# Stage 1 of a two-weight spectral filter in four row tiles, with x loaded in quarters of the partitions from two queues

## The chip, the cores and the metric

The kernel runs on one core of a Trainium2 chip. A core has a matrix engine (PE, with its weight loads shown separately as PEld), a vector engine (DVE), a scalar engine (ACT), a general engine (POOL) and a queue engine (SP), each with its own instruction stream, and sixteen DMA engines that they share. On-chip memory is SBUF (128 partitions); PE writes to PSUM, which has eight banks of 512 float32 values per partition. The metric is device time of one execution in microseconds (us). Of three timed runs of the kernel before, the median is 121.32 us (121.32 to 121.65).

## The reference

One input x of 2048 rows by 1024 columns, two complex weight arrays of 2048 by 513, one gate vector of 1024. All are bf16; the transforms are computed in float32.

```python
def f(x, w_r, w_i):
    X = rfft2(x.astype(float32))
    X = X * (w_r + 1j * w_i)
    return irfft2(X, s=(2048, 1024)).astype(bfloat16)

x = A_x
g = sigmoid((x * gate_w).sum(-1, keepdims=True))
out = g * f(x, A_w_r, A_w_i) + (1 - g) * f(x, B_w_r, B_w_i)
```

Both filters are applied to the same x, so the forward transform is made once.

## The kernel before, in words

The two transforms are split into stages that are matrix products with constant matrices. The 2048 rows of x are taken as 32 times 64: a row's number is 64 n1 + 16 b + r, with n1 from 0 to 31, b from 0 to 3 and r from 0 to 15. Stage 1 is the transform over n1. Stage 2 is the transform along the columns, stage 4 the one over the 64 values of (b, r). Products with the weights follow on DVE (L504), stage 5 (L600) begins the way back, and stages 6 and 7 make the output rows.

x is loaded as 128 partitions of 16 consecutive rows: partition p = 4 n1 + b holds rows 16 p to 16 p + 15, one after the other. The loads go in four chunks c of four values of r, each in the parts that XPARTS (L293) lists, all on SP's queue. A constant M of 128 by 2048 (L46) holds, for each r, a 128 by 128 matrix that applies the transform over n1 to all four b at once: in the row of a partition with one b, the columns of the other three b are zero. M comes in three loads (`mload`, L299), the first on ACT's queue. After x and M, SP issues F2, the gate row, CK, SM and then the 44 loads of the weights (`wload`, L319), in the order in which they are used.

Before stage 1, each part of x is folded on DVE (`fold`, L333): sums (h = 0) and differences (h = 1) of columns d and 1023 - d, 256 columns at a time (s = 0, 1), into XF, which holds two chunks. `negate` (L354) makes the negated M: chunks 0 and 1 on ACT, 2 and 3 on DVE.

`stage1(c)` (L364) makes for each (h, j) of a chunk a unit of two PSUM banks. For each of its four r, two matmuls (s = 0, 1) accumulate 256 columns, M and its negative side by side; the stationary operand is 128 columns of the folded x. When a unit is complete, ACT copies it as bf16 into FT (L391), 1024 elements per partition; two of the sixteen units are copied by DVE (L389), and the very last is copied in two pieces, the first 32 of its 128 columns alone. The tag "F1a" lets the first work of stage 2 (`fold3`, L432, on DVE, and `stage2`, L442) start when that first piece is copied.

The program keeps for every engine the order in which instructions are written, and waits by semaphores for what each instruction reads or overwrites. So a matmul that waits for folded x holds back every later matmul, and an eviction that waits holds back every later ACT instruction. Steps 0 to 15 then follow (`step`, L643): stage 4 of one piece, an exchange of real and imaginary halves by DMA (`swap`, L487, on POOL's queue, for the later pieces on SP's, behind the weight loads), stage 2 of the next piece but one, and products. A stage-4 result goes into one of seven buffers, which come free when the products that read them are done.

Of the kernel before, what the change touches and what calls it, by code (L numbers as in the profile page):

```python
# [6 lines left out]
ALU = mybir.AluOpType  # L7
# [17 lines left out]
def make_consts():  # L25
# [20 lines left out]
    C["M"] = M.reshape(128, 2048)  # L46
# [186 lines left out]
def bass_gated_mix__spectral_gfnet__spectral_gfnet__prompt_kernel(nc, A_x, A_w_r, A_w_i, B_x, B_w_r, B_w_i, gate_w, out):  # L233
# [46 lines left out]
    xv = x2.rearrange("(p r) d -> p (r d)", r=16)  # L280
# [12 lines left out]
    XPARTS = {0: ((0, 1), (1, 1), (2, 2)), 1: ((0, 2), (2, 2)), 2: ((0, 2), (2, 2)), 3: ((0, 2), (2, 2))}  # L293
# [5 lines left out]
    def mload(eng, c0, n):  # L299
        load(f"M{c0}", MM, c0 * 512, n * 512, cst["M"].ap()[:, c0 * 512:(c0 + n) * 512], eng=eng, w=[("M", c) for c in range(c0, c0 + n)])  # L300

    mload("act", 0, 1)
    for c in range(4):
        t, o = xloc(c)
        for q0, n in XPARTS[c]:
            dma("sp", f"x{c}{q0}", sl(t, o + q0 * 1024, [(1, n * 1024)]), xv[:, (4 * c + q0) * 1024:(4 * c + q0 + n) * 1024], w=[("x", c, q0)])
        if c < 2:
            mload("sp", 1 + c, 1 + c)
# [3 lines left out]
    P.add("act", lambda e: e.activation(sl(DUM, 1, [(1, 1)]), sl(DUM, 0, [(1, 1)]), ACT.Sigmoid), r=["DUM"], w=["DUM2"])  # L312
# [41 lines left out]
    def negate(c, n=1, eng="act"):  # L354
        dst, src = sl(MM, 2048 + c * 512, [(1, n * 512)]), sl(MM, c * 512, [(1, n * 512)])
        kw = dict(r=[("M", k) for k in range(c, c + n)], w=[("NM", k) for k in range(c, c + n)])
        if eng == "dve":
            P.add("dve", lambda e: e.tensor_scalar(out=dst, in0=src, scalar1=-1.0, scalar2=None, op0=ALU.mult), **kw)
        else:
            P.add("act", lambda e: e.activation(dst, src, ACT.Copy, scale=-1.0), **kw)  # L360

    cnt = 0

    def stage1(c):  # L364
        nonlocal cnt
        us = [(cnt + k) % 4 for k in range(4)]
        cnt += 4
        parts = XPARTS[c] if c == 0 else ((0, 4),)
        for q0, n in parts:
            for h in range(2):  # L370
                for j in range(2):
                    u = us[2 * h + j]
                    for q in range(q0, q0 + n):
                        r = 4 * c + q
                        base = (c % 2) * 4096 + q * 1024 + h * 512
                        o = ps(u * 1024 + q * 256, [(1, 256)])
                        for s in range(2):
                            lh = sl(XF, base + 256 * s + 128 * j, [(1, 128)])
                            rh = sl(MM, r * 128, [(2048 * s, 2), (1, 128)])
                            P.add("pe", lambda e, o=o, lh=lh, rh=rh, s=s: e.matmul(o, lh, rh, start=(s == 0), stop=(s == 1)),  # L380
                                  r=[("xf", c % 2, q, h, s ^ j), ("M", c), ("NM", c)], w=[bank(2 * u + q // 2)])
                    if q0 + n < 4:
                        continue
                    for m0, mn in ((0, 32), (32, 96)) if (c, h, j) == (3, 1, 1) else ((0, 128),):
                        src = ps(u * 1024 + m0, [(128, 2), (1, mn), (256, 4)])
                        dst = sl(FT, h * 8192 + j * 2048 + 16 * m0 + 4 * c, [(4096, 2), (16, mn), (1, 4)])
                        kw = dict(r=[bank(2 * u), bank(2 * u + 1)], a=[("F1", h, j)] + [("F1a", h, j)] * (m0 == 0))
                        if (c, h, j) in ((2, 1, 1), (3, 0, 1)):
# [5 lines left out]
    negate(1)  # L394
    folds(0)
    folds(1)
    negate(2, 2, "dve")
    stage1(0)
    stage1(1)
    fold(2, 0, 2, 0)  # L400
# [520 lines left out]
```

## Time and profile before

| what | us |
|---|---|
| median of three runs | 121.32 |
| the profiled execution, its own time | 121.57 |
| span of its trace | 119.4 |
| stage 1, first fold to last eviction | 4.71 to 22.07 |
| PE busy | 110.0 |
| DVE busy | 97.4 |
| ACT busy | 98.8 |

The trace is of one execution, so sums made from its rows are compared with 121.57 us. PE's ends are modelled, because matmuls overlap in the array: a row's duration is from the start of an instruction to its result, and the spacing of starts tells the rate. The waits name what an engine waited for last. "SPq" and "ACTq" are the time in which an engine's queue issued a DMA; the transfer itself is told apart from it.

### The profile page before, as it was taken

Reading aid. Unit: us, or ns where it says so; the run is one execution under the profiler, and the core shown is the slowest. Engines: PE = TensorE matmul, PEld = TensorE weight load, DVE = VectorE, ACT = ScalarE, POOL = GpSimd, SP = SyncE. Lnnn points to the kernel's source line nnn. Section 1 sums busy time; section 2 is a strip of 40 time slices with the busy share of each in tenths; the row PEclk is TensorE's granted clock in tenths of the full one; section 3 lists DMA queues with packets and bytes.
Section 4 is the critical chain, followed back from the end, with each engine's and each line's share of the span. In section 5 each row is a group of like instructions: output and inputs, shape, how many; then the busy total and the mean of one; then the engine's idle time right before and its main releaser. Section 6 shows DMA issues by size and latency. Waiting matters only on the chain.

```text
span 119.4 us, 4238 instructions
## 1 busy us (share of the span) xinstructions
PE 110.0 (92%) x1812; PEld 88.2 (74%) x1812; DVE 97.4 (82%) x202; ACT 98.8 (83%) x119; POOL 33.9 (28%) x43
## 2 busy tenths in 40 slices
PE   6789999999999999889999999999889899999950
PEld 4566889887665766378999999999877667877420
DVE  0478998985999999999999997994537868999980
ACT  4239998999799999849999999996878968889720
POOL 1000030026664600000000000000006979789940
PEclk9999999999999999999999999999999999999999
DMA  2999999999999999844599800000000242442546
GB/s 89 314 347 412 422 379 354 350 348 349 366 362 371 361 364 363 315 150 144 128 328 401 294 4 5 0 0 5 0 5 0 96 181 88 181 176 93 206 173 236
DMA packets 17683, 26.14 MB, mean 219 GB/s; under 512 B 2113, under 2 KB 11073, under 8 KB 17665
## 3 DMA queue, kind: packets, MB, share of 16 engines
q1 hardware_dynamic: 16368, 23.00, 55.3%
q0 software_dynamic: 864, 2.36, 5.4%
q10 hardware_dynamic: 432, 0.52, 1.3%
q8 instruction: 14, 0.23, 0.8%
q14 instruction: 5, 0.03, 0.1%
HBM read 17.48 MB, written 4.19 MB: 182 GB/s over the span
## 4 chain that ended last, share of the span: by engine, by line
PE 30%; SPq 28%; POOL 12%; DMA 8%; DVE 8%; issue 6%; ACT 3%; POOLq 1%; DVEq 0%; ACTq 0%
SPq L284 28%; PE PS L600 25%; POOL MM L829 9%; DMA W<-in_B_w_i_dram 5%; DMA W<-in_A_x_dram 3%; POOL XF L829 3%; DVE W L504 3%; DVE FT L824 2%; PE PS L380 2%; DVE MM L788 2%; POOLq L860 1%; PE PS L748 1%; PE PS L777 1%; PE PS L477 1%; ACT XF L485 1%
## 5 line engine op out<-in xcount | busy, mean ns | idle before, releaser
L600 PE MATMUL PS<-CL,W 128*128 128x128 bf16 x512 | 32.4, 225 | 0.3 <-DVE W L504 0.2
L600 PEld LDWEIGHTS PS<-CL,W 128*128 128x128 bf16 x512 | 31.7, 145 | 1.3 <-DVE W L504 0.9
L829 POOL TENSOR_TENSOR MM<-FT 128x512 bf16<-128x512 f32 x14 | 17.5, 1277 | 50.9 <-DVE FT L824 50.9
L611 ACT ACTIVATE W<-PS 128x1024 bf16<-128x1024 f32 (+1 forms) x30 | 28.5, 1036 | 1.2 <-PE PS L600 1.1
L504 DVE TENSOR_TENSOR W<-XF,W 128x1024 bf16<-128x1024 bf16 (+2 forms) x36 | 22.1, 631 | 1.3 <-ACT XF L485 1.1
L504 DVE TENSOR_TENSOR W<-MM,W 128x1024 bf16<-128x1024 bf16 (+2 forms) x36 | 22.0, 636 | 0.4 <-DMA MM<-XF 0.2
L777 PE MATMUL PS<-FT,W 128*128 128x256 bf16 (+1 forms) x132 | 20.0, 302 | 0.9 <-DVE MM L788 0.4
L761 ACT ACTIVATE W<-PS 128x1024 bf16<-128x1024 f32 (+1 forms) x16 | 15.8, 994 | 3.5 <-PE PS L748 3.3
L477 PE MATMUL PS<-XF,CK 128*128 128x512 bf16 (+1 forms) x72 | 17.5, 357 | 0.8 <-ACT XF L485 0.8
L485 ACT ACTIVATE XF<-PS 128x1024 bf16<-128x1024 f32 x15 | 16.2, 1078 | 2.5 <-DVE W L504 2.1
L466 ACT ACTIVATE XF<-PS 128x1024 bf16<-128x1024 f32 x16 | 17.1, 1076 | 0.6 <-PE PS L460 0.5
L777 PEld LDWEIGHTS PS<-FT,W 128*128 128x128 bf16 x132 | 12.1, 98 | 6.7 <-DVE MM L788 0.7
L341 DVE TENSOR_TENSOR XF<-W 128x512 bf16<-128x512 bf16 (+2 forms) x34 | 11.4, 403 | 6.2 <-DMA W<-in_A_x_dram 5.9
L380 PE MATMUL PS<-MM,XF 128*128 128x256 bf16 x128 | 14.9, 273 | 1.5 <-DVE XF L341 1.4
L380 PEld LDWEIGHTS PS<-MM,XF 128*128 128x128 bf16 x128 | 12.2, 98 | 4.2 <-DVE XF L341 2.7
L391 ACT ACTIVATE FT<-PS 128x1024 bf16<-128x1024 f32 (+2 forms) x15 | 13.1, 1012 | 0.9 <-PE PS L380 0.9
L284 POOL DMA_DIRECT2D MM<-XF x18 | 9.9, 551 | 13.7 <-PE PS L477 8.1
L824 DVE TENSOR_TENSOR FT<-PS,XF 128x512 f32<-128x512 f32 x18 | 11.5, 683 | 2.3 <-ACT XF L784 2.1
L451 PEld LDWEIGHTS PS<-F,FT 128*128 128x128 bf16 x128 | 8.4, 98 | 3.1 <-ACT FT L391 0.2
L784 ACT ACTIVATE XF<-PS 128x512 f32<-128x512 f32 (+1 forms) x16 | 8.8, 547 | 1.9 <-PE PS L777 1.9
L451 PE MATMUL PS<-F,FT 128*128 128x128 bf16 x128 | 10.2, 219 | 0.0
L477 PEld LDWEIGHTS PS<-XF,CK 128*128 128x128 bf16 x72 | 4.8, 97 | 6.5 <-ACT XF L485 5.4
(63 smaller groups left out, 100.4 us busy)
## 6 DMA issues: line engine op xcount, KB each, us to landing
W<-in_A_x_dram SPq DMA_DIRECT2D x7, 512.0 KB, 7.6
out_dram<-MM SPq DMA_DIRECT2D x10, 256.0 KB, 2.7
MM<-XF POOLq DMA_DIRECT2D x18, 128.0 KB, 5.3
FT<-c_U SPq DMA_DIRECT2D x1, 2048.0 KB, 9.5
MM<-XF SPq DMA_DIRECT2D x14, 128.0 KB, 2.5
W<-in_A_w_r_dram SPq DMA_DIRECT2D x4, 256.5 KB, 6.1
W<-in_A_w_i_dram SPq DMA_DIRECT2D x4, 256.5 KB, 6.6
W<-in_B_w_r_dram SPq DMA_DIRECT2D x4, 256.5 KB, 7.0
```

Source lines behind the costliest of these rows:

```text
L284: return P.add(eng, lambda e: e.dma_start(dst, src), dma=name, **kw)
L380: P.add("pe", lambda e, o=o, lh=lh, rh=rh, s=s: e.matmul(o, lh, rh, start=(s == 0), stop=(s == 1)), r=[("xf", c % 2, q, h, s ^ j), ("M", c ...
L451: P.add("pe", lambda e, o=o, cs=cs, j=j, t=t, rh=rh: e.matmul(o, fblock(1 + cs, j, t), rh, start=(j == 0), stop=(j == 1)), r=[("F1a" if p ...
L466: P.add("act", lambda e: e.activation(dst, src, ACT.Copy), **kw)
L477: P.add("pe", lambda e, o=o, kind=kind, pm=pm, m=m, rh=rh: e.matmul(o, sl(CK, fbo(kind, pm, m), [(1, 128)]), rh, start=(m == 0), stop=(m = ...
L485: P.add("act", lambda e: e.activation(dst, src, ACT.Copy), **kw)
L504: P.add("dve", lambda e: e.tensor_tensor(out=rows((1 - h) * 64 * RP + sw * HW), in0=sl(xt, xo + 128 * h + 64 * h0, [(0, 2), (256, 4 * ni), ...
L600: P.add("pe", lambda e, o=o, l0=l0, ab=ab: e.matmul(o, sl(W, HW * ab + l0, [(RP, 128)]), sl(CL, KIo[ab], [(1, 128)]), start=(ab == 0), sto ...
L611: P.add("act", lambda e: e.activation(dst, src, ACT.Copy), r=b, a=keys)
L761: P.add("act", lambda e, s=src, d=dst: e.activation(d, s, ACT.Copy), **kw)
L777: P.add("pe", lambda e: e.matmul(ps(col, [(1, n * 256)]), lh, rh, start=(k == 0), stop=(k == last)), r=[("Y", r), "DI"] + ["DJ"] * (full o ...
L829: P.add("pool", lambda e, s=s, op=op: e.tensor_tensor(out=ods(s, 0, 2), in0=pv[:, :, 0, :], in1=pv[:, :, 1, :], op=op), r=[("PQ", pk, 0), ...
```

## The change

x is loaded in another layout: partition 32 b + n1 holds rows 64 n1 + 16 b to 64 n1 + 16 b + 15, so each b has 32 partitions of its own. A part of a chunk is now four transfers of 32 partitions, one for each b (g in the code); those of b = 2 and 3 are issued by ACT for chunks 0 to 2, and all four by SP for chunk 3. Chunk 2 is one part of four rows instead of two parts of two. M keeps only the columns of its partition's own b, so it is 128 by 512 instead of 128 by 2048, comes in one load on ACT's queue, and is negated once, on DVE, ahead of the first fold. The activation that brings the table for Sigmoid moves behind ACT's loads of chunk 1.

Stage 1 takes 32 partitions at a time: 512 matmuls with 32 rows and 64 columns instead of 128 with 128 rows and 256 columns, consecutive ones on different quarters of the rows. A call has four banks, one for each b, and two calls alternate. There are eight calls: two rows r with both h in chunk 0, and four rows with one h in the other chunks. After each call come two evictions of two banks, 1024 elements each, fifteen on ACT and one on DVE (chunk 3, h = 0). The tag "F1a" and the copy in two pieces are gone.

```diff
-    C["M"] = M.reshape(128, 2048)
+    C["M"] = M.sum(-1).swapaxes(0, 1).reshape(128, 512)
...
-    xv = x2.rearrange("(p r) d -> p (r d)", r=16)
+    xsrc = lambda r, n, g: AP(x2.tensor, x2.offset + (16 * g + r) * D, [[64 * D, 32], [1, n * D]])
...
-    XPARTS = {0: ((0, 1), (1, 1), (2, 2)), 1: ((0, 2), (2, 2)), 2: ((0, 2), (2, 2)), 3: ((0, 2), (2, 2))}
+    XPARTS = {0: ((0, 1), (1, 1), (2, 2)), 1: ((0, 2), (2, 2)), 2: ((0, 4),), 3: ((0, 2), (2, 2))}
...
-    def mload(eng, c0, n):
-        load(f"M{c0}", MM, c0 * 512, n * 512, cst["M"].ap()[:, c0 * 512:(c0 + n) * 512], eng=eng, w=[("M", c) for c in range(c0, c0 + n)])
-
-    mload("act", 0, 1)
+    load("M", MM, 0, 512, cst["M"].ap(), eng="act", w=["M"])
     for c in range(4):
         t, o = xloc(c)
         for q0, n in XPARTS[c]:
-            dma("sp", f"x{c}{q0}", sl(t, o + q0 * 1024, [(1, n * 1024)]), xv[:, (4 * c + q0) * 1024:(4 * c + q0 + n) * 1024], w=[("x", c, q0)])
-        if c < 2:
-            mload("sp", 1 + c, 1 + c)
+            for g in (0, 2, 1, 3):
+                dma("act" if g > 1 and c < 3 else "sp", f"x{c}{q0}", sl(t, o + q0 * 1024, [(1, n * 1024)], p0=32 * g, np_=32), xsrc(4 * c + q0, n, g),
+                    **({"a": [("x", c, q0)]} if g else {"w": [("x", c, q0)]}))
+        if c == 1:
+            P.add("act", lambda e: e.activation(sl(DUM, 1, [(1, 1)]), sl(DUM, 0, [(1, 1)]), ACT.Sigmoid), r=["DUM"], w=["DUM2"])
...
-    def negate(c, n=1, eng="act"):
...
+    P.add("dve", lambda e: e.tensor_scalar(out=sl(MM, 512, [(1, 512)]), in0=sl(MM, 0, [(1, 512)]), scalar1=-1.0, scalar2=None, op0=ALU.mult), r=["M"], w=["NM"])
     cnt = 0
 
-    def stage1(c):
+    def stage1(c, q0, nq, hs, engs):
+
         nonlocal cnt
...
+        s0 = 4 * (cnt % 2)
+        cnt += 1
+        w = 128 * len(hs)
+        for q in range(q0, q0 + nq):
+            for h in hs:
                 for j in range(2):
...
+                    for s in range(2):
+                        for g in range(4):
+                            lh = sl(XF, (c % 2) * 4096 + q * 1024 + h * 512 + 256 * s + 128 * j, [(1, 128)], p0=32 * g, np_=32)
+                            rh = sl(MM, (4 * c + q) * 32, [(512 * s, 2), (1, 32)], p0=32 * g, np_=32)
+                            o = ps((s0 + g) * 512 + (q - q0) * w + (h - hs[0]) * 128 + j * 32, [(64, 2), (1, 32)])
                             P.add("pe", lambda e, o=o, lh=lh, rh=rh, s=s: e.matmul(o, lh, rh, start=(s == 0), stop=(s == 1)),
...
+        for g, eng in zip((0, 2), engs):
+            src = ps((s0 + g) * 512, [(512, 2), (1, w), (w, nq)])
+            dst = sl(FT, hs[0] * 8192 + 16 * g + 4 * c + q0, [(16, 2), (64, w), (1, nq)])
...
-    negate(0)
-    negate(1)
     folds(0)
     folds(1)
-    negate(2, 2, "dve")
-    stage1(0)
-    stage1(1)
-    fold(2, 0, 2, 0)
-    fold(2, 2, 2, 0)
-    fold(2, 0, 4, 1)
+    for q0 in (0, 2):
+        stage1(0, q0, 2, (0, 1), ("act", "act"))
+    for hh in range(2):
+        stage1(1, 0, 4, (hh,), ("act", "act"))
+    folds(2)
     folds(3)
-    stage1(2)
-    stage1(3)
+    for hh in range(2):
+        stage1(2, 0, 4, (hh,), ("act", "act"))
+    for hh in range(2):
+        stage1(3, 0, 4, (hh,), ("act", ("dve", "act")[hh]))
```

More of the change, by code (lines that the diff above doesn't have):

```diff
@@ L311, in bass_gated_mix__spectral_gfnet__spectral_gfnet__prompt_kernel @@
     load("CK", CK, 0, 1056, cst["CK"].ap(), w=["CK", "GW2"])
-    P.add("act", lambda e: e.activation(sl(DUM, 1, [(1, 1)]), sl(DUM, 0, [(1, 1)]), ACT.Sigmoid), r=["DUM"], w=["DUM2"])
     dma("sp", "SM", SM[:], cst_sm.ap(), w=["SM"])
@@ L352, in folds @@
             fold(c, q0, n, h)
-    def negate(c, n=1, eng="act"):
[L355 to L360, printed above, removed]
+    P.add("dve", lambda e: e.tensor_scalar(out=sl(MM, 512, [(1, 512)]), in0=sl(MM, 0, [(1, 512)]), scalar1=-1.0, scalar2=None, op0=ALU.mult), r=["M"], w=["NM"])
@@ L362, in bass_gated_mix__spectral_gfnet__spectral_gfnet__prompt_kernel @@
     cnt = 0
-    def stage1(c):
+    def stage1(c, q0, nq, hs, engs):
         nonlocal cnt
[L366 to L370, printed above, removed]
-                for j in range(2):
[L372 to L388, printed above, removed]
-                            P.add("dve", lambda e, s=src, d=dst: e.tensor_copy(d, s), **kw)
-                        else:
-                            P.add("act", lambda e, s=src, d=dst: e.activation(d, s, ACT.Copy), **kw)
@@ L393, in bass_gated_mix__spectral_gfnet__spectral_gfnet__prompt_kernel @@
-    negate(0)
-    negate(1)
+        s0 = 4 * (cnt % 2)
[3 more added lines that the diff above has]
+            for h in hs:
+                for j in range(2):
+                    for s in range(2):
[3 more added lines that the diff above has]
+                            o = ps((s0 + g) * 512 + (q - q0) * w + (h - hs[0]) * 128 + j * 32, [(64, 2), (1, 32)])
+                            P.add("pe", lambda e, o=o, lh=lh, rh=rh, s=s: e.matmul(o, lh, rh, start=(s == 0), stop=(s == 1)),
+                                  r=[("xf", c % 2, q, h, s ^ j), "M", "NM"], w=[bank(s0 + g)])
@@ new lines, in stage1 @@
+        for g, eng in zip((0, 2), engs):
+            src = ps((s0 + g) * 512, [(512, 2), (1, w), (w, nq)])
+            dst = sl(FT, hs[0] * 8192 + 16 * g + 4 * c + q0, [(16, 2), (64, w), (1, nq)])
+            kw = dict(r=[bank(s0 + g), bank(s0 + g + 1)], a=[("F1", h, j) for h in hs for j in range(2)])
+            if eng == "dve":
+                P.add("dve", lambda e, s=src, d=dst: e.tensor_copy(d, s), **kw)
+            else:
+                P.add("act", lambda e, s=src, d=dst: e.activation(d, s, ACT.Copy), **kw)
@@ L438, in fold3 @@
             P.add("dve", lambda e, dst=dst, src=src, op=op: e.tensor_tensor(out=dst, in0=src[0], in1=src[1], op=op),
-                  r=[("F1a" if i < 2 else "F1", cs, j) for cs in css for j in range(2)] + [("FR", i, j) for j in range(2)],
+                  r=[("F1", cs, j) for cs in css for j in range(2)] + [("FR", i, j) for j in range(2)],
                   w=[("E", i, cs, s) for cs in css] + [("FR", i - 2, s)] * (i > 1))
@@ L451, in stage2 @@
                         P.add("pe", lambda e, o=o, cs=cs, j=j, t=t, rh=rh: e.matmul(o, fblock(1 + cs, j, t), rh, start=(j == 0), stop=(j == 1)),
-                              r=[("F1a" if p < 2 else "F1", cs, j), "F2"], w=[bank(b0 + t % 2)])
+                              r=[("F1", cs, j), "F2"], w=[bank(b0 + t % 2)])
         if 1 in ab:
```

## The prediction

> **What bounds the kernel now.** I read the page's busy shares first: PE 92%, ACT 83%, DVE 82%, an average over stages, so it names no bound. The slices of DMA traffic come next; the first and third lines below show stages 1 to 4 with the sixteen DMA engines full. The windows answer gives the rate: 363 GB/s while x and the constants load (2 to 15 us), 359 GB/s while the weights load (18 to 48 us).
>
> ```profile
> DMA  2999999999999999844599800000000242442546
> GB/s 89 314 347 412 422 379 354 350 348 349 366 362 371 361 364 363 315 150 144 128 328 401 294 4 5 0 0 5 0 5 0 96 181 88 181 176 93 206 173 236
> ...
> 2.00:15.00 13.00, 11.52 (x91) 8.82 (x90) 8.80 (x27) 8.38 (x12) 0.00 (x0) 1.00 0.99 363
> 18.00:48.00 30.00, 29.96 (x461) 21.48 (x459) 27.48 (x56) 28.50 (x33) 9.88 (x18) 1.00 1.08 359
> ```
>
> Then the chain of work that ended last. From 7 to 43 us it is SP issuing loads; the last weight load lands at 48.88 us and a product on DVE starts 0.05 us later; then DVE, ACT and from 54.55 us PE, without a hole to 85.7 us.
>
> ```profile
> 43.06 5.78 DMA W<-in_B_w_i_dram
> 48.88 0.04 issue
> 48.93 0.78 DVE W L504 x2
> 49.73 0.45 DVE W L504
> 50.20 2.13 DVE W L504 x6
> 52.38 0.05 issue
> 52.43 1.03 ACT XF L485
> 53.46 0.05 issue
> 53.51 1.04 PE PS L477 x4
> 54.55 10.79 PE PS L600 x176
> ```
>
> The DVE timeline shows what that chain hides: DVE runs products back to back from 31.18 us, and the one starting at 48.93 waited about 0.2 us where its neighbours start 0.1 us late anyway. So two chains arrive together at 49 us: the loads, and the compute chain that began with stage 1. The loads are later by about 0.1 us. A change to stage 1 shifts the end by the later of the two.
>
> What sets stage 1 itself is read from the ACT timeline: evictions one after the other.
>
> ```profile
> 7.48 0.63 ACT L360 ACTIVATE MM<-MM 128x512 bf16<-128x512 bf16 x1 [2.32 <-DMA MM<-c_M]
> 8.49 11.11 ACT L391 ACTIVATE FT<-PS 128x1024 bf16<-128x1024 f32 x12 [0.38 <-PE PS L380]
> 20.07 2.00 ACT L391 ACTIVATE FT<-PS 128x1024 bf16<-128x1024 f32 x3 [0.47 <-PE PS L380]
> 21.94 0.20 ACT L514 ACTIVATE CK<-PS 128x8 bf16<-128x8 f32 x1
> ```
>
> Twelve in 11.11 us with a last one of 1.06 us is a step of 0.914 us. PE is nearly as full there: eight matmuls an eviction at 256 columns, 92 of them in 10.45 us, 0.91 us per eviction. It is a tie, so a faster PE alone gives stage 1 little.
>
> **Bytes.** x is 4.194 MB and M was 0.524 MB; M becomes 0.131 MB. Before 2 us 0.03 MB had moved (windows of 1 us). Before: 4.69 MB in 12.9 us at 363 GB/s. After: 4.29 MB. At the same 363 it would take 11.8 us, 1.1 less. But each x transfer now covers 32 partitions, from two queues, and the trace has no such transfer of any size. Bounds: as fast as now (-1.1 us), or, if a quarter of the partitions reaches only half of what the engines can write, 182 GB/s: 23.6 us (+10.7). The nearest row is the weight loads: 64 partitions, 128 to 256 KB each, rows of a strided source, 359 GB/s; the x pieces are 64 to 256 KB. I take 350 for the smaller pieces: 12.3 us, 0.6 less. Everything behind x on the queues (F2, the gate row, CK, SM, 44 weight loads) moves with it, since the DMA engines never run dry: SP issues 20 x pieces where it issued seven loads of x and two of M in some 5.8 us. At 0.43 us each (median of its x issues) they take 8.6 us, so the first weight load is issued at about 11.1 us instead of 8.41. By then some 3.2 of 5.0 MB are moved, 5 us of work is queued, and this lateness costs nothing; if transfers were to drain faster than they are issued it would cost up to 2.7 us. The gate row's copy on POOL (16.84 us, 1.15 long) follows its load; PE's first instruction after stage 1 needs it at 20.6, so 2.6 us of lateness would show nowhere.
>
> [...]
>
> **ACT.** Removed: two negations of 0.63 us, both ahead of the first eviction and in waiting time, so nothing. Added ahead of the evictions: twelve x issues. M is issued by 1.10 us (0.35 us row); ten issues at 0.40 (between that row and SP's 0.43) to 5.1; the table load of 1.28 and the activation of 0.20, now behind them, to 6.6; two more issues, 7.4 if they wait for the table load, 6.6 if not. The first call (x rows 0 and 1) could be evicted when its last piece is in: issued at 2.3 us, landing after between 1.8 us (the XST row) and 4.0 us (the two 256 KB loads), 4.1 to 6.3, I take 5.5; four folds at 0.21 (eight took 1.70) 6.4; matmuls 0.6: 7.0. So the evictions begin at 7.2 us (6.6 to 8.5) instead of 8.49. ACT does 15 whole evictions where it did the work of 14: one goes from DVE to ACT. Same 1024 elements, so the same 0.914 and 1.06: 7.2 + 14 x 0.914 + 1.06 = 21.06 us. Behind the issues nothing but evictions waits on ACT; PE waits for those through the banks.
>
> **The tail.** Before, the first quarter of the last eviction alone let the second half's folds for stage 2 start: eight took 1.77 us from 20.52, a step of 0.21, the fifth at 21.37 us. Now both evictions of the last call must end: 21.06 + 0.05. That is 0.3 us earlier.
>
> **PE.** 128 matmuls of 256 columns become 512 of 64 columns on 32 rows. Nearest row: stage 6, 64 matmuls of 64 rows by 64 columns start 1.04 us apart as a block.
>
> ```profile
> 88.66 1.11 PE L748 MATMUL PS<-FT,W 64*128 64x64 bf16 x64
> 89.70 2.35 PE L777 MATMUL PS<-FT,W 128*128 128x256 bf16 x16
> ```
>
> 16.2 ns each with two row tiles; L460's full rows at 64 columns take 32.5 (eight in 0.26). Four tiles: 8.1 if they scale, 32.5 if not; I take at most 16.2, or 1.04 us a call against 1.83 us of evictions. PE is then idle half of stage 1, which is worth nothing while ACT sets the pace. At 32.5 it is 2.08 a call: PE is the bound.
>
> **DVE.** One negation of 512 instead of 1024 (0.42 us, at most) now comes before the first fold and waits for M, which is first on its queue (landing 4.5 us before): hidden by the wait for x, at worst 0.4 us into ACT's slack. One eviction less, 1.22 us; the other is done before ACT's. Folds are the same elements; those of chunk 3 need x complete by about 16 us (ACT reaches it at 18.2), at 350 GB/s it is in by 14.3. The clock was granted at 1.0 in every window.
>
> **Sum.** Compute chain -0.3; with the loads 0.6 earlier the 0.1 us on DVE goes too: -0.4 us. Against the profiled execution, 121.57 us (span 119.4, 2.2 outside): 121.2. The median of the runs is 121.32: 120.9 us. About 0.3% (0.36 us) is what a measurement can tell from no change, so this is only just outside.
>
> **Rivals.**
> x loads slower than now. The end follows the loads, us for us: they decide from 4.29 MB in 13.3 us, 323 GB/s, and below this it is slower. For it: smaller pieces, each in a quarter of the partitions, and the last 1 MB from SP alone. Against: the weight loads on half the partitions hold 359. At 290: 14.8 us, +1.9, 123.2 us. [...]
> ACT held by its issues. If an issue takes 0.6 us (the weight loads on SP do), ten take 6 instead of 4 and the last two 1.2: evictions from 9.8, +2.2 us, 123.5. It is slower once the first eviction starts after 7.96 us. Against: simple issues cost 0.35 to 0.45.
> Row tiles that do not run side by side: seven calls of 2.08 from 8.0 us to 22.6, two evictions 1.97: 24.5 against 21.37, 124.4 us. Against: the stage 6 row.
> Nothing measurable: first eviction between 7.3 and 7.96 us; the gain is the tie of PE and ACT in stage 1, 121.2.
>
> **How the numbers follow.** Forecast 0.43. Nothing measurable 0.14. x loads at 250 to 323 GB/s 0.20, half rate 0.10, ACT late 0.08, row tiles one by one 0.05. So faster 0.43, same 0.14, slower 0.43. The lower end: evictions from 6.6 us, -1.0, 120.3, and a little, 120.2. The upper end 125.0 takes in row tiles one by one and loads down to 259 GB/s; left out are half rate (0.10) and some 0.08 at both ends. The likeliest case's own range is 120.2 to 121.0.
>
> **What the profile after would show.** Loads right: 345 GB/s or more from 2 to 14 us and the last weight landing before 48.5; wrong: slices under 320 there and DVE waiting for weights at 44 to 52 us. ACT right: first eviction at 7.2, steps of 0.91, no idle time until 21. PE right: matmul blocks of under 1.05 us with idle time behind each. Slower evictions, or a granted clock below 1.0 now that PE is half idle, would be causes that I leave out of the sum.

## The result

The kernel after takes 132.57 us (median of four runs, 131.89 to 134.21), the one before on the same chip 121.41 us. The ratio is 1.090 (95% interval 1.083 to 1.097), without the slowest of the four runs of after, which was in a slower state: 9% slower, far outside the range of 120.2 to 125.0. The profiled execution of after took 132.03 us with a span of 129.8, against 121.57 and 119.4: 10.4 us to explain.

### The profile page after: what moved, and what is told of

The parts are those of the page before. It is cut to its first block, busy times and chain, and to the rows that moved or that the text cites. A ratio compares the mean times of both kernels' runs of the same rounds, so it can differ in the third digit from the quotient of the medians.

```text
span 129.8 us, 5020 instructions
## 1 busy us (share of the span) xinstructions
PE 109.3 (84%) x2196; PEld 86.8 (67%) x2196; DVE 96.2 (74%) x199; ACT 99.1 (76%) x117; POOL 34.0 (26%) x43
## 4 chain that ended last, share of the span: by engine, by line
PE 53%; DVE 20%; issue 8%; ACT 7%; DMA 6%; ACTq 3%; DVEq 0%
PE PS L586 23%; DVE W L490 14%; PE PS L763 12%; DMA W<-in_A_x_dram 6%; PE PS L734 5%; PE PS L463 4%; ACT FT L378 4%; PE PS L369 4%; ACTq L284 3%; PE PS L437 2%; DVE MM L774 2%; PE PS L446 1%; DVE XF L469 1%; DVE XF L339 1%; PE PS L504 1%
## 5 line engine op out<-in xcount | busy, mean ns | idle before, releaser
L369 PE MATMUL PS<-MM,XF 32*128 32x64 bf16 x512 | 11.8, 227 | 12.1 <-issue 6.0
L378 ACT ACTIVATE FT<-PS 128x1024 bf16<-128x1024 f32 x15 | 14.4, 1029 | 9.1 <-PE PS L369 9.1
L369 PEld LDWEIGHTS PS<-MM,XF 32*128 32x128 bf16 x512 | 8.8, 114 | 15.4 <-issue 7.0
L463 PE MATMUL PS<-XF,CK 128*128 128x512 bf16 (+1 forms) x72 | 18.3, 372 | 0.8 <-ACT XF L471 0.8
L471 ACT ACTIVATE XF<-PS 128x1024 bf16<-128x1024 f32 x15 | 16.2, 1078 | 3.1 <-DVE W L490 1.6
L437 PE MATMUL PS<-F,FT 128*128 128x128 bf16 x128 | 11.4, 236 | 1.2 <-ACT FT L378 1.2
L437 PEld LDWEIGHTS PS<-F,FT 128*128 128x128 bf16 x128 | 9.3, 106 | 4.4 <-ACT FT L378 1.4
```

The costliest lines, as they stand in the source:

```text
L378: P.add("act", lambda e, s=src, d=dst: e.activation(d, s, ACT.Copy), **kw)
L437: P.add("pe", lambda e, o=o, cs=cs, j=j, t=t, rh=rh: e.matmul(o, fblock(1 + cs, j, t), rh, start=(j == 0), stop=(j == 1)), r=[("F1", cs, j ...
L463: P.add("pe", lambda e, o=o, kind=kind, pm=pm, m=m, rh=rh: e.matmul(o, sl(CK, fbo(kind, pm, m), [(1, 128)]), rh, start=(m == 0), stop=(m = ...
L471: P.add("act", lambda e: e.activation(dst, src, ACT.Copy), **kw)
```

## The profile after

Three lines of the slices of after (40 slices of 3.25 us; PEclk is the granted clock of the matrix engine in tenths, 9 is 90% or more):

```profile
PEclk9985555555599999999999999999999999999997
DMA  3899999999999999443226992000000025443447
GB/s 114 279 313 294 283 286 347 353 347 322 336 349 322 340 293 364 162 151 134 86 83 175 402 393 90 0 5 0 5 0 5 0 88 209 173 146 129 167 158 246
```

Two things are new. From the fourth to the eleventh slice, 10 to 36 us, the matrix engine has half its clock. And the second to sixth slices move 279 to 313 GB/s where the kernel before reached 314 to 422, though the DMA engines are as full. The windows give both as means (columns: stretch, length, busy time of PE, PEld, DVE, ACT and POOL with counts, then clock, DMA share and GB/s):

```profile
2.00:15.00 13.00, 8.47 (x219) 5.24 (x217) 6.34 (x21) 5.77 (x7) 0.00 (x0) 0.76 0.96 289
18.00:48.00 30.00, 22.81 (x513) 17.64 (x510) 18.47 (x45) 22.35 (x25) 7.86 (x13) 0.70 1.05 337
```

289 GB/s instead of 363 while x loads, at a share of 0.96 instead of 0.99: the engines are as busy and move a fifth fewer bytes.

The evictions of stage 1 in the timeline of ACT (start, length, what, count, and in brackets the idle time before with its releaser):

```profile
7.84 1.98 ACT L378 ACTIVATE FT<-PS 128x1024 bf16<-128x1024 f32 x2 [0.43 <-PE PS L369]
11.38 1.97 ACT L378 ACTIVATE FT<-PS 128x1024 bf16<-128x1024 f32 x2 [1.57 <-PE PS L369]
14.66 1.94 ACT L378 ACTIVATE FT<-PS 128x1024 bf16<-128x1024 f32 x2 [1.31 <-PE PS L369]
18.50 3.77 ACT L378 ACTIVATE FT<-PS 128x1024 bf16<-128x1024 f32 x4 [1.90 <-PE PS L369]
24.30 2.86 ACT L378 ACTIVATE FT<-PS 128x1024 bf16<-128x1024 f32 x3 [2.03 <-PE PS L369]
29.02 1.94 ACT L378 ACTIVATE FT<-PS 128x1024 bf16<-128x1024 f32 x2 [1.86 <-PE PS L369]
```

The first starts at 7.84 us, 0.65 earlier than before, and each still takes its 0.9 to 1.0 us. But where the kernel before had twelve in a row without a gap, ACT now stands idle ahead of every group, 9.1 us in all, always for PE. The last one ends at 30.96 us instead of 22.07. So 8.9 of the 10.4 us are lost inside stage 1, and the engine that sets it is no longer ACT. The other 1.5 us come behind stage 1; the section on the experiments returns to them with the half clock.

What PE waited for is in its own timeline:

```profile
13.21 1.30 PE L369 MATMUL PS<-MM,XF 32*128 32x64 bf16 x44 [1.44 <-DVE XF L339]
16.56 2.66 PE L369 MATMUL PS<-MM,XF 32*128 32x64 bf16 x116 [2.05 <-issue]
19.67 0.23 PE L369 MATMUL PS<-MM,XF 32*128 32x64 bf16 x2 [0.45 <-ACT FT L378]
20.49 0.34 PE L369 MATMUL PS<-MM,XF 32*128 32x64 bf16 x9 [0.59 <-ACT FT L378]
23.35 1.77 PE L369 MATMUL PS<-MM,XF 32*128 32x64 bf16 x117 [2.52 <-issue]
25.47 0.23 PE L369 MATMUL PS<-MM,XF 32*128 32x64 bf16 x2 [0.34 <-ACT FT L378]
26.30 0.29 PE L369 MATMUL PS<-MM,XF 32*128 32x64 bf16 x8 [0.59 <-ACT FT L378]
28.06 0.92 PE L369 MATMUL PS<-MM,XF 32*128 32x64 bf16 x54 [1.47 <-issue]
```

Until 15 us PE waits for folded x. Then come three waits put down to "issue": no semaphore that the profile knows was missing. Two of them fall inside a call, after nine matmuls and after eight, so they are no waits for data. Count the matmuls from one to the next: 116 + 2 + 9 = 127, and 117 + 2 + 8 = 127. The first comes after 64 + 64 + 32 + 44 = 204 matmuls of stage 1. A hole at the same count, whatever place of the work it falls on, suggests that the engine ran out of instructions; the experiments test it. 127 matmuls with their weight loads are 254 instructions. The chain that ended last shows the same three holes, and then the old work, shifted (start, length, what):

```profile
14.51 2.05 issue
...
20.83 2.52 issue
...
26.59 1.47 issue
...
65.38 10.81 PE PS L586 x176
```

That last row stood at 54.55 us before: +10.8. The weights no longer matter; in their place this chain runs through DVE's products without a transfer in it.

The page counts the transfers that bring instructions as a queue of their own. Of the kernel before (packets, MB, share):

```profile
q8 instruction: 14, 0.23, 0.8%
```

and of after:

```profile
q8 instruction: 17, 0.28, 0.9%
```

A packet is 0.28 MB / 17, about 16.5 KB. Stage 1 went from 128 to 512 matmuls, which with their weight loads is 768 more instructions; three more packets of 256 are 768. So a packet holds 256 instructions by estimate, and the 254 from one hole to the next are nearly one packet. Up to the first hole PE ran the 18 matmuls at the program's start (L297) and 204 of stage 1, 444 instructions with their loads; why the first hole comes there is not shown.

## The experiments

Theory I: PE consumes its 512 small matmuls faster than the instruction queue delivers them while the DMA engines are full; the half clock follows from the holes (the second half of this did not hold, see below). Theory L: the slower loads of quarters set stage 1. The table gives the outcome; every ratio is to the kernel before in the same job.

| kernel | median us | ratio (95%) | x, 2 to 15 us, GB/s | PE waits put to issue in stage 1, us |
|---|---|---|---|---|
| after | 132.57 | 1.090 (1.083 to 1.097) | 289 | 6.0 |
| after_whole_loads | 130.19 | 1.067 (1.060 to 1.074) | 361 | 6.0 |
| before_quarter_loads | 126.55 | 1.040 (1.036 to 1.045) | 275 | 0 |
| after_two_tiles | 126.55 | 1.041 (1.035 to 1.048) | 287 | 0 |
| before_split_columns | 128.48 | 1.056 (1.050 to 1.063) | 375 | 3.9 |
| two_tiles_contiguous_loads | 122.10 | 1.002 (0.998 to 1.005) | 394 | 0 |

**One cause at a time.** after_whole_loads is the kernel after with x loaded as before, so that rows stand in other partitions than the row tiles assume; the instructions from stage 1 on are those of after:

```diff
-            for g in (0, 2, 1, 3):
-                dma("act" if g > 1 and c < 3 else "sp", f"x{c}{q0}", sl(t, o + q0 * 1024, [(1, n * 1024)], p0=32 * g, np_=32), xsrc(4 * c + q0, n, g),
-                    **({"a": [("x", c, q0)]} if g else {"w": [("x", c, q0)]}))
+            dma("sp", f"x{c}{q0}", sl(t, o + q0 * 1024, [(1, n * 1024)]), xv[:, (4 * c + q0) * 1024:(4 * c + q0 + n) * 1024], w=[("x", c, q0)])
```

> The changed kernel with x loaded as before: transfers of 128 partitions from SP alone, no x transfer from ACT. The rows then stand in other partitions than the four row tiles assume, so the output is not the reference's; all instructions of stage 1 and after are those of the changed kernel. Theory I (PE runs out of instructions: with the DMA engines full, a block of some 256 PE instructions takes 5 to 7 us to arrive, and 512 matmuls with their 512 weight loads use one up in 2 us; the idle PE then drops to the half clock): loads are back at about 363 GB/s, but the holes of 1.5 to 2.5 us that PE spends on 'issue' in stage 1 stay, the clock falls to 0.5 all the same, and the time is 127 to 131 us. Theory L (the slower quarter loads, 290 GB/s from 2 to 17 us, set the length of stage 1): 121 to 123 us, no holes.

x came at 361 GB/s again, the three holes stayed after the same counts (116, 2 + 9, 117, 2 + 8), and so did the half clock (0.50 in the mean of 17 to 30 us). Loads alone are not the cause.

before_quarter_loads is the reverse: the kernel before, with x in quarters from two queues. As in the change, the activation for Sigmoid moves behind ACT's loads of chunk 1; those lines are not printed here.

```diff
-            dma("sp", f"x{c}{q0}", sl(t, o + q0 * 1024, [(1, n * 1024)]), xv[:, (4 * c + q0) * 1024:(4 * c + q0 + n) * 1024], w=[("x", c, q0)])
+            for g in (0, 2, 1, 3):
+                dma("act" if g > 1 and c < 3 else "sp", f"x{c}{q0}", sl(t, o + q0 * 1024, [(1, n * 1024)], p0=32 * g, np_=32), xsrc(4 * c + q0, n, g),
+                    **({"a": [("x", c, q0)]} if g else {"w": [("x", c, q0)]}))
```

> The kernel before with x alone loaded as in the change: four transfers of 32 partitions for each part, those of the upper two quarters from ACT for chunks 0 to 2. M with its zeros and the 128 matmuls of 256 columns stay; the rows stand in other partitions than M assumes, so the output is not the reference's. Theory I: 4.69 MB at 290 GB/s take 16.2 us instead of 12.9, so the weights land 3.3 us later: 123 to 126 us, no hole on 'issue' in PE's stage 1, clock 1.0. Theory L: 130 to 133 us.

Its first window and its evictions:

```profile
2.00:15.00 13.00, 9.23 (x56) 6.52 (x55) 6.42 (x21) 4.81 (x7) 0.00 (x0) 0.87 0.98 275
```

```profile
12.93 11.11 ACT L394 ACTIVATE FT<-PS 128x1024 bf16<-128x1024 f32 x12 [3.12 <-PE PS L383]
24.34 2.00 ACT L394 ACTIVATE FT<-PS 128x1024 bf16<-128x1024 f32 x3 [0.30 <-PE PS L383]
```

The evictions run without a hole again and are 4.3 us later; the last weight landed at 53.47 instead of 48.88, the span grew by 4.7. So quarters cost 4% by themselves, and the span grew by about as much as the last weight came later.

after_two_tiles keeps the quarters and halves the number of matmuls: two row tiles of 64 partitions, two b in each, 256 matmuls of 128 columns. M is then 128 by 1024, half of it zeros.

```diff
-                        for g in range(4):
+                        for g in range(2):
...
-                            rh = sl(MM, (4 * c + q) * 32, [(512 * s, 2), (1, 32)], p0=32 * g, np_=32)
+                            rh = sl(MM, (4 * c + q) * 64, [(1024 * s, 2), (1, 64)], p0=64 * g, np_=64)
```

> The changed kernel with two row tiles of 64 rows instead of four of 32: 256 matmuls of 128 columns, M with half zeros (128 x 1024); x loads as in the change; everything is computed. Theory I: half the PE instructions, 512 in stage 1, so the holes are fewer and shorter: 123 to 128 us. Theory L: M is 0.13 MB longer and the loads are the same, so 132 to 133 us.

No wait on PE is put down to issue and the granted clock is 1.0 in every window to 20 us. The queue of instructions has 15 packets, one more than before, for 256 instructions more. Stage 1 ends at 26.31, and the whole kernel costs what the quarters alone cost.

**Is it the number of instructions, or the row tiles?** before_split_columns has neither row tiles nor new loads, only each matmul cut in four by columns:

```diff
-                        for s in range(2):
+                        for k in range(4):
+                            for s in range(2):
+                                o = ps(u * 1024 + q * 256 + 64 * k, [(1, 64)])
...
+                                rh = sl(MM, r * 128 + 2048 * s * (k // 2) + 64 * (k % 2), [(1, 64)])
```

> The kernel before with each of the 128 matmuls of stage 1 cut in four of 64 columns (512 matmuls on all 128 rows; same loads, same constants, same evictions): the number of instructions of the kernel after without its row tiles and without its loads. By theory I the number of instructions alone brings the waits for instructions: PE shows waits put down to issue inside stage 1, about 127 matmuls apart, of 1.5 to 2.5 us each, and the time is 124 to 129 us. Rival, the row tiles themselves bring them: no such waits, and matmuls at 32.5 ns each (512 take 16.6 us where 128 took 13.9 with 11.7 us of busy time) make PE the bound of stage 1 by about 2.7 us: 124.0 us, with PE back to back and the clock at 1.0.

PE's timeline:

```profile
5.34 7.01 PE L381 MATMUL PS<-MM,XF 128*128 128x64 bf16 x204 [0.66 <-DVE XF L341]
13.79 3.88 PE L381 MATMUL PS<-MM,XF 128*128 128x64 bf16 x127 [1.43 <-issue]
19.99 5.42 PE L381 MATMUL PS<-MM,XF 128*128 128x64 bf16 x127 [2.33 <-issue]
25.57 1.75 PE L381 MATMUL PS<-MM,XF 128*128 128x64 bf16 x54 [0.16 <-issue]
```

204, 127, 127, 54: the same counts as in the kernel after, without row tiles and with whole loads. So the holes go with the number of matmuls, as theory I has it. The arrival of an instruction is in no row of the traces; what follows reads the holes by that theory. Blocks arrive 6.2 and 5.6 us apart here, 6.8 and 4.7 in the kernel after. By that reading a block of 127 matmuls must last that long or PE waits. In before it lasts 127 x 0.114 = 14.5 us (eight matmuls in 0.91); with two tiles, 32 matmuls in ACT's 1.83, it lasts 7.3 us, just enough; with four, 64 in 1.83, it is 3.6 us.

**What makes a block slow?** after_weights_held makes the weights' loads wait until the last matmul of stage 1.

```diff
-                    dma("sp", f"w{key}", d, s, a=[("W", key)])
+                    dma("sp", f"w{key}", d, s, a=[("W", key)], after=[P.ops["pe"][-1]])
```

> The changed kernel with the 44 weight loads held until the last matmul of stage 1 is done, so that the DMA engines have nothing but x, F2, the gate row, CK and SM until then. The whole is longer, since the weights come later; only stage 1 is looked at. Theory I: once x has landed the blocks of instructions arrive quickly: the holes on 'issue' after 18 us (2.5 and 1.5 us) shrink below 0.7 us each and the last eviction of stage 1 ends 2 to 4 us earlier than 30.96 us. Theory L, or a limit of PE's own issue: the holes stay and stage 1 ends at 30 to 31 us.

A single execution took 137.71 us, since the weights come late. PE's timeline at the first two blocks:

```profile
17.55 2.66 PE L369 MATMUL PS<-MM,XF 32*128 32x64 bf16 x116 [2.63 <-issue]
...
22.70 1.77 PE L369 MATMUL PS<-MM,XF 32*128 32x64 bf16 x117 [0.88 <-issue]
```

The first hole, with x still loading, is no shorter (2.63 us, 2.05 in the kernel after); the second shrank from 2.52 to 0.88, the third went. PE's own pace between the first hole and the second was the same (4.3 us for these 127 matmuls in both kernels). From 17 to 30 us the DMA engines moved 83 GB/s at a share of 0.31 here, and 344 GB/s at 1.09 from 18 to 30 us in the kernel after. So, by this one execution, the other transfers lengthen the arrival of a block. It is still 5.2 us here, part of it beside x; the time of a block with nothing beside it is not shown.

**How much is the half clock?** after_fillers puts four long matmuls ahead of each call from the second on, to keep PE busy:

```diff
+        for _ in range(4 if cnt > 1 else 0):
+            P.add("pe", lambda e: e.matmul(ps(s0 * 512, [(1, 512)]), sl(MM, 0, [(1, 128)]), sl(MM, 0, [(1, 512)]), start=True, stop=True),
+                  r=["M"], w=[bank(s0)])
```

> The kernel after with four matmuls of 128 rows by 512 columns of M, whose results are overwritten, ahead of each of the calls of stage 1 from the second on (28 more matmuls, nothing else). What it tells apart: how much of the 10.6 us that the change costs is PE's halved clock, and how much the waits for instructions. Theory I with the clock as a side effect: the fillers keep PE busy ahead of the calls, the granted clock rises from 0.50 to near 1.0 in stage 1, the three waits for instructions stay (about as long, 1.5 to 2.5 us each), and the time falls by 1 to 3 us, to 129.5 to 131.5. Rival, the clock is the cause of most of the loss: with the clock near 1.0 the last eviction of stage 1 ends by 25 us instead of 30.96, and the time is 126 us or less. If the clock stays at 0.50 all the same, the run says nothing on its price and the time is 132 to 134.

134.5 us, ratio 1.103 (1.097 to 1.109). The clock came back for about 3 us and fell again; slices of 3.34 us:

```profile
PEclk9995955559959999999999999999999999999998
```

In windows of 3 us it was 0.59 from 9 to 12 us, 0.84 and 0.73 in the next two, 0.50 from 18 to 30 and 0.99 from 30 to 33. The run gives no price of the clock. Its PE timeline is worth having all the same:

```profile
24.35 0.24 PE L372 MATMUL PS<-MM,XF 32*128 32x64 bf16 x3 [2.72 <-issue]
24.52 1.89 PE L362 MATMUL PS<-MM 128*128 128x512 bf16 x4
26.34 1.04 PE L372 MATMUL PS<-MM,XF 32*128 32x64 bf16 x64
27.31 1.89 PE L362 MATMUL PS<-MM 128*128 128x512 bf16 x4
29.13 0.92 PE L372 MATMUL PS<-MM,XF 32*128 32x64 bf16 x53
30.82 0.26 PE L372 MATMUL PS<-MM,XF 32*128 32x64 bf16 x11 [0.76 <-issue]
...
31.98 0.68 PE L372 MATMUL PS<-MM,XF 32*128 32x64 bf16 x64
```

The fillers count: 3 + 4 + 64 + 4 + 53 = 128 matmuls between two holes, at other places of the program. And 64 small matmuls take 0.68 us once the clock is back, against 1.04 at half clock: 10.6 ns each, where two row tiles took 16.2 and full rows 32.5. Four row tiles do run side by side.

The other runs say more of the half clock. It cannot come from the holes alone: in the kernel after it was at 0.50 by 9 us, and the first hole began at 14.5; before_quarter_loads, without a hole, had it from about 9 to 12 us; before_split_columns, with holes at the same counts, kept 1.00 in the mean of 2 to 20 us; its mean of 0.986 over 125.9 us leaves, by estimate, some 3 us at 0.50 after that. What sets it off stays open. It does not set the pace of the blocks either: in before_split_columns they came 6.2 us apart while the clock was 1.00, in the kernel after 6.8 and 4.7 us apart at 0.50, so a slower PE mostly used up time that it would have waited. Behind stage 1 it does cost. The clock of the kernel after was back only at 36 us, and eight matmuls of 256 columns took, before and after that, in the chain of this kernel:

```profile
33.56 1.73 PE PS L463 x8
...
40.26 0.97 PE PS L463 x8
```

Kernels with a low clock there lost more in the span than in stage 1, after 1.5 us and after_whole_loads 2.7; those with a full clock there lost little more, before_quarter_loads 0.4, after_two_tiles 0.2, before_split_columns 0.1. This compares different kernels; no run changes the clock alone.

**The loads.** Two variants ask what makes them slow. before_quarters_sp is before_quarter_loads with all quarters issued by SP:

```diff
-                dma("act" if g > 1 and c < 3 else "sp", f"x{c}{q0}", sl(t, o + q0 * 1024, [(1, n * 1024)], p0=32 * g, np_=32), xsrc(4 * c + q0, n, g),
+                dma("sp", f"x{c}{q0}", sl(t, o + q0 * 1024, [(1, n * 1024)], p0=32 * g, np_=32), xsrc(4 * c + q0, n, g),
```

> The kernel before with x loaded in quarters of 32 partitions, as in the run with two queues, but all of them from SP's queue alone (rows stand in other partitions, so the output is not the reference's). What it tells apart: whether the 275 GB/s of that run come from the quarters or from having two queues. If the transfers of 32 partitions themselves are slower, the x phase is as slow or slower, 200 to 275 GB/s, and the time is 126.5 us (275) to 132 (200). If the two queues got in each other's way, the rate is back above 320 GB/s and the time is 121.5 to 123.5. SP's 28 x issues at 0.43 us (12 us) put a floor of about 350 GB/s under neither.

two_tiles_half_loads is the kernel with two tiles, each part of x in two halves of 64 partitions, one from each queue (in chunk 3 both from SP):

```diff
-            for g in (0, 2, 1, 3):
+            for g in (0, 1):
...
+    xsrc = lambda r, n, g: AP(x2.tensor, x2.offset + (16 * g + r) * D, [[32 * D, 64], [1, n * D]])
```

> Two row tiles of 64, as in the run with two tiles (256 matmuls of stage 1 on 64 rows by 128 columns, M 128 by 1024), but x is loaded in halves of 64 partitions, one from each queue, in place of quarters. If what made the loads slow is that a transfer covers only 32 of 128 partitions and that doubling this doubles its share, the rate is back near 350 GB/s and, with no waits for instructions, the time is 120.8 to 121.8 us, level with the kernel before or better. If 64 neighbouring partitions load no faster than quarters did (275 to 290), it is 126 to 127 us, as with quarters. [...]

The first window of quarters from SP:

```profile
2.00:15.00 13.00, 9.30 (x54) 6.00 (x53) 5.13 (x18) 5.55 (x8) 0.00 (x0) 0.95 0.77 240
```

and of halves from two queues:

```profile
2.00:15.00 13.00, 8.29 (x101) 5.53 (x101) 5.36 (x18) 5.39 (x6) 0.00 (x0) 0.71 0.98 269
```

One queue is worse (240 GB/s, engines no longer full at 0.77; 132.48 us, ratio 1.088), so two queues helped. Not all of that time is the loads' own: from 14 to 20 us the clock was 0.50 in this run, and evictions came 1.71 us apart behind PE instead of 0.91. Halves are no better than quarters (269; 126.17 us, ratio 1.037). What holds transfers to a part of the partitions at 240 to 289 GB/s is not shown.

**Both causes away.** The first attempt kept the rows where two tiles need them and loaded all 128 partitions at once, from a source of three dimensions (the second run has the last eviction on DVE):

```diff
+    xsrc = lambda r, n: AP(x2.tensor, x2.offset + r * D, [[16 * D, 2], [32 * D, 64], [1, n * D]])
...
+            dma("sp", f"x{c}{q0}", sl(t, o + q0 * 1024, [(1, n * 1024)]), xsrc(4 * c + q0, n), w=[("x", c, q0)])
```

> Both causes removed and the rest of the change kept: two row tiles of 64 (256 matmuls on 64 rows by 128 columns in place of 512 on 32 by 64, M 128 by 1024), and each part of x in one transfer to all 128 partitions, from SP's queue, eight in all, with a source of three dimensions that puts the rows of b = 0 and 2 in the first 64 partitions and those of b = 1 and 3 in the others. If the number of PE's instructions and the transfers that cover a part of the partitions are the whole cause, no wait on PE is put down to issue, the clock stays at 1.0, the x phase runs at 350 to 366 GB/s, and the time is 120.6 to 122.0 us: level with the kernel before, within about 0.5%, since the first eviction can start at about 8 us, fifteen steps of 0.914 us follow and end at about 22. If the rest of the change (fewer and longer waits of an eviction, four banks a call, no last eviction in two pieces) has a price of its own, the time is 122.5 to 124. If a source of three dimensions is slower than rows that follow each other, the x phase shows it, under 330 GB/s.

> As the run with two row tiles and whole loads, with the second eviction of the very last call on DVE as well (beside the first one on ACT) instead of behind it on ACT: ACT makes fourteen evictions, DVE two. The last eviction ends some 0.7 us earlier (0.914 for one ACT eviction less, the one on DVE takes 1.22 instead of 1.02), and the time is 0.4 to 0.8 us less than without this if stage 1 sets the end there; the same within 0.3 us if the weights' transfers set it by then (the last landed at 48.88 us in the kernel before, 0.1 us from binding; 0.26 MB less of M is worth 0.7 us to them).

191.13 and 191.45 us: a miss of another kind. From 30 to 60 us of the first:

```profile
30.00:60.00 30.00, 4.13 (x64) 3.24 (x64) 2.86 (x8) 3.77 (x4) 0.00 (x0) 0.50 0.13 54
```

54 GB/s at a share of 0.13. That is by estimate the share of two engines of sixteen (0.125), and the outermost dimension of this source is 2; that the one comes from the other is the author's guess, since no run tries another such source. The next run puts the question again, with contiguous rows:

```diff
-            dma("sp", f"x{c}{q0}", sl(t, o + q0 * 1024, [(1, n * 1024)]), xsrc(4 * c + q0, n), w=[("x", c, q0)])
+            dma("sp", f"x{c}{q0}", sl(t, o + q0 * 1024, [(1, n * 1024)]), xv[:, (4 * c + q0) * 1024:(4 * c + q0 + n) * 1024], w=[("x", c, q0)])
```

> As the run with two row tiles and whole loads, but each part of x comes as in the kernel before, 16 consecutive rows to each partition (so rows stand in other partitions and the output is not the reference's). The source of three dimensions of that run was spread over two of the sixteen DMA engines (a share of 0.13 from 15 to 60 us) and so told nothing on the question it was made for; this one puts it again. If the number of PE's instructions and the transfers to part of the partitions are the whole cause, x comes at 350 to 366 GB/s, no wait on PE is put down to issue, the clock is 1.0, and the time is 120.6 to 122.0 us. If something else in the change costs, 122.5 to 124.

Ratio 1.0015 (0.998 to 1.005): with 256 matmuls and whole loads the rest of the change is worth nothing measurable. Its evictions:

```profile
6.90 12.26 ACT L377 ACTIVATE FT<-PS 128x1024 bf16<-128x1024 f32 x13 [4.28 <-PE PS L368]
19.35 1.94 ACT L377 ACTIVATE FT<-PS 128x1024 bf16<-128x1024 f32 x2 [0.19 <-PE PS L368]
```

They start at 6.90 and end at 21.29, 0.8 us ahead of the kernel before: the shape that the prediction had in mind. The twelve executions part by the granted clock. The four with a mean of 0.998 or more took 120.61 to 121.16 us, the eight with 0.968 to 0.986 took 121.80 to 122.98; the kernel before shows no such difference (medians of 121.35 with 0.998 or more and 121.45 below). In the profiled execution, one of the eight, the clock was 1.00 from 2 to 15 us and 0.89 in the mean of 15 to 30 us. PE idles 0.2 to 0.6 us behind most calls here; that this is what costs the clock is a guess. The sound part of the change needs x at full rate in a layout that the one full-width transfer tried here did not give, so no kernel of this study computes the reference faster than the one before.

**Was the bound read rightly?** The prediction rests on two chains that meet at 49 us, loads and stage 1. Five runs tried to shorten them in the kernel before without row tiles. The first two write M without its zeros and let POOL put them back by a product with a mask; chunk 0's evictions take two rows r and both h:

```diff
+    for c in range(1, 4):
+        P.add("pool", lambda e, c=c: e.tensor_tensor(out=sl(MM, 512 * c, [(4, 128), (1, 4)]), in0=sl(MM, 4608 + 128 * (c - 1), [(1, 128), (0, 4)]),
+              in1=sl(MM, 4992, [(0, 128), (1, 4)]), op=ALU.mult), r=["MC"], w=[("M", c)])
...
-        parts = XPARTS[c] if c == 0 else ((0, 4),)
+        parts = ((0, 2), (2, 2)) if c == 0 else ((0, 4),)
...
-            for h in range(2):
+            for hs in ((0, 1),) if c == 0 else ((0,), (1,)):
```

> What of the change stands the test, put into the kernel before without its row tiles and without its quarters: x and the 128 matmuls of 128 rows by 256 columns as before; of M the zeros are left out for chunks 1 to 3 (384 columns and four of a mask, 0.10 MB in place of 0.39, on ACT's queue) and POOL, idle until 16 us, puts them back (three products with the mask, about 1.3 us each by its row for 128 by 512); and chunk 0's units cover two rows r and both h in place of four rows and one h, so that the first eviction needs rows 0 and 1 alone. If the two chains that met at 49 us are still the bound, the loads are 0.29 MB shorter, 0.8 us at 363 GB/s, and the first eviction comes 1 to 1.5 us earlier (7.0 to 7.5 instead of 8.49): 120.4 to 120.9 us, a ratio of 0.992 to 0.997. [...]

132.34 us, ratio 1.085 (1.080 to 1.091), by an error of order: the products stood behind POOL's copy of the gate row and started at 16.46 us; ACT waited 13.0 us for them, with every eviction behind. Written ahead of that copy, and then each half alone:

> As the run with the small constants, with POOL's three products written ahead of its copy of the gate row, so that they run as soon as the 384 columns and the mask are in (about 3.5 to 8 us). Two chains that tie: loads 0.29 MB or 0.8 us shorter, first eviction 1 to 1.5 us earlier, the smaller of the two is gained: 120.5 to 121.0 us, a ratio of 0.992 to 0.997. No gain (121.2 to 121.7) if something that neither touches sets the end. Slower (122 or more) if POOL's products delay chunk 1, or DVE beside them.

> The smaller M with POOL's products, and chunk 0's units as in the kernel before: the loads are 0.8 us shorter, stage 1 is as before (its first eviction at about 8.5 us, or up to 0.4 earlier since x comes sooner). If the two chains tie, the gain is 0.1 to 0.4 us: 121.0 to 121.4. If the loads alone bind it is 0.8: 120.6.

> Chunk 0's units of two rows and both h alone, M loaded as before: the first eviction comes 1 to 1.5 us earlier, the loads are unchanged. If the two chains tie with the loads 0.1 us later, nothing is gained: 121.2 to 121.6, and the trace shows DVE waiting for the last weights at 48.9 us for as much as stage 1 gained. If stage 1 alone binds it is about 120.4.

Units alone: 121.32 us, ratio 0.999 (0.996 to 1.002). In the profiled execution stage 1 ended 0.6 us earlier (21.51) and DVE's run of products began 0.55 us earlier (30.63 instead of 31.18), until it stood still for weights; the chain, below, has the last weights in it:

```profile
42.12 0.69 DVE L505 TENSOR_TENSOR W<-XF,W 128x1024 bf16<-128x1024 bf16 x1 [0.88 <-DMA W<-in_B_w_i_dram]
...
43.09 6.16 DMA W<-in_B_w_i_dram
49.34 0.78 DVE W L505 x2
```

The last product starts 0.09 us behind the landing. What stage 1 gained went into waiting for the loads, as a tie with the loads ahead foretold; this execution took 122.68 us, the longest of twelve, and its last weights landed 0.37 us later than before. Constants alone: 122.26 us, ratio 1.005 (1.003 to 1.007); both: 124.0, 1.019 (1.014 to 1.024). Here POOL is in the way. With constants alone, in POOL's timeline:

```profile
4.79 3.20 POOL L315 TENSOR_TENSOR MM<-MM 128x512 bf16<-128x512 bf16 x3 [3.70 <-DMA MM<-c_MC]
```

and in DVE's:

```profile
4.10 8.26 DVE L344 TENSOR_TENSOR XF<-W 128x256 bf16<-128x256 bf16 x20 [4.10 <-DMA W<-in_A_x_dram]
```

Twenty folds that took 1.70 + 2.33 + 2.10 = 6.13 us of busy time before take 8.26; the longest is 1.12 us instead of 0.42, about the length of one product on POOL. So stage 1 ended at 23.00, 0.9 later. The last attempt had no work on POOL: DVE clears M's place before the first fold, and four transfers bring each b to its partitions.

```diff
+    P.add("dve", lambda e: e.memset(sl(MM, 0, [(1, 2048)]), 0.0), w=["MZ"])
+    for b in range(4):
+        dma("act", "M", sl(MM, 512 * b, [(1, 512)], p0=b, np_=32, pstep=4).bitcast(u16), AP(cst["M"].ap().tensor, b * 512, [[2048, 32], [1, 512]]), r=["MZ"], a=[("M", c) for c in range(4)])
...
-                            o = ps(u * 1024 + col, [(1, 256)])
+                            o = ps(u * 1024 + col, [(128, 2), (1, 4), (4, 32)])
```

> The run with chunk 0's units of two rows and both h, and M loaded without zeros: DVE clears 2048 columns before its first fold, four transfers on ACT's queue each bring the 512 columns of one b to its 32 partitions (every fourth), the matmul reads them with a stride and writes the same columns of PSUM as before. 0.39 MB less to load, 1.1 us at 363 GB/s, and no product on POOL. If the end is set by two chains that tie at 49 us, and the first eviction comes at about 7.4 us as in the run with units alone (it ended stage 1 0.7 us earlier), the smaller part is gained: 120.5 to 120.9 us, a ratio of 0.992 to 0.996. If strides on PE's operands cost time, stage 1's matmuls are longer than 0.91 us per eight and the time is above 121.5.

141.08 us, ratio 1.161 (1.157 to 1.165). The four transfers behind x landed only at 10.8 us, and evictions then come 1.73 us apart, since eight matmuls with a strided result and a strided operand take that long instead of 0.91, at a granted clock of 1.00 from 15 to 48 us. Which stride it is was not tried. That fewer bytes together with an earlier stage 1 gain 0.5 us or more stays unshown.

## Why the prediction was wrong

- **PE.** This is the step that failed: "PE is then idle half of stage 1, which is worth nothing while ACT sets the pace". Its price was right (at most 1.04 us a call; 0.68 at full clock). What it left out is where the instructions come from: four times as many, in the same time. By theory I, PE waited 6.0 us for them in three holes; ACT waited 9.1 us for PE, so ACT did not set the pace. The half clock, named there as a cause left out of the sum, came too; the 1.5 us lost behind stage 1 are its likely share, not separated by a run of its own. Together with quarters the number of matmuls, with the half clock that came along, costs about 6 us (ratio 1.090 against 1.041), with whole loads about 8 (1.067 against 1.002): part of one wait hides behind the other.
- **Bytes.** The term of 350 GB/s measured 289, below the 323 at which the forecast turned to slower. (By the prediction's own terms the loads decide from 12.5 us, 343 GB/s, since the compute chain ends 0.4 us earlier; 323 is where the loss is clear of noise.) The rival of slower loads was right in kind and short in size: it gave 123.2 us at 290, and after_two_tiles, which has only this fault, took 126.55 at 287. It counted the bytes on the way to the weights; but stage 1 itself waited for the quarters and ended 4.2 us later: in that run the first fold started at 5.96 us instead of 4.71, and behind it DVE waited 4.3 us for x instead of 1.2. The bound of half rate, 182 GB/s and 10.7 us more, comes near the result by chance: no run with quarters shows that rate (240 from one queue, 275 to 289 from two), and the missing 6 us are PE's.
- **The rates as bounds.** The weight loads on every second partition, taken as the nearest row, did not stand for 32 neighbouring partitions: 359 GB/s there, 289 here.
- **ACT.** Ten issues took 4.74 us, not 4.0; the first eviction came at 7.84, not 7.2. Small, and covered. The rival of ACT held by its issues did not decide.
- **SP.** Its twenty issues took 10.06 us, not 8.6, and the first weight load went out at 12.88 us, not 11.1. (The kernel before issued nine loads of x in those 5.8 us; the prediction read seven, which are those of 512 KB alone.) The DMA engines stayed full from 8 to 30 us, so this lateness shows no cost of its own, as forecast.
- **Row tiles one by one.** This rival was wrong, as the prediction held: 64 in 0.68 us.
- **The bound.** The tie of two chains at 49 us holds as far as it was tested: an earlier stage 1 alone gained nothing and met a wait for weights of 0.88 us. The gain of 0.4 us was there at most in the executions at full clock of two_tiles_contiguous_loads, the kernel with neither fault.

## What to carry to other kernels

Before splitting matmuls into smaller ones, divide: 127 matmuls with their weight loads, as theory I reads the holes, arrived every 5 to 7 us here while the DMA engines were full, 18 to 25 per us. By estimate from this, a stage that runs more than some 20 matmuls per us for longer than two blocks starves, however idle PE looks: with two tiles, 17 per us, no wait of PE was put down to issue; with four, which wanted 35 per us, it waited 6.0 us. Read a wait put down to "issue" by counting the instructions between two of them. And price a transfer by a row that covers the same partitions: 32 or 64 neighbours moved 240 to 289 GB/s where all 128 moved 361 to 394, and from two queues the DMA engines were just as busy.

## What the runs showed of the hardware that was not expected

- Instructions come in packets of about 16.5 KB on a DMA queue of their own; 768 more instructions of PE brought three more packets, and holes 127 matmuls apart (128 with the fillers), with or without row tiles. With fewer transfers beside it a hole shrank from 2.52 to 0.88 us, in a single execution.
- The granted clock fell to 0.50 by 9 us in the kernel after, where the longest gap of PE until then was 1.54 us (7.18 to 8.72). In after_fillers it stayed there through 5.7 us of nearly gapless matmuls (24.35 to 30.05 us) before it rose.
- A load whose source has an outermost dimension of 2 ran at 54 GB/s, with the DMA engines at a share of 0.13.
- Beside elementwise products on POOL, DVE's folds took as much as 1.12 us where the longest of the same twenty took 0.42 in the kernel before.
